# A convolution and a mixture of experts in one kernel, with the written-out order of all its steps made anew

## The chip, the cores and the metric

One core of one Trainium2 chip runs the whole program. The metric is device time in microseconds, the median of three runs: 1271.48 us for the kernel before (1271.06 to 1281.67).

## What is computed

The reference chains two parts, for 8 sequences of 3584 tokens with 192 channels, all in float32.

```
w = softmax(weight_gen, over 7 taps)                       # per token and head, 8 heads of 24 channels
out[b, s] = sum_k w[b, s, k] * x_pad[b, s + k]             # a causal convolution whose taps depend on the token
logits = out @ w_gate + modality_bias[modality_id]         # 8 experts
e = argmax(logits);  gate = softmax(logits)[e]
y = gate * (relu(out @ w1[e]) @ w2[e])                     # 192 -> 1024 -> 192, the chosen expert alone
```

The first three lines and the routing are called attention below, the last one pages.

## The kernel before

**Units and pages.** The 28672 tokens are worked on in 16 units of 1792 (128 partitions of 14 tokens), each unit in two halves of 7 tokens. A unit's rows, once convolved and routed, are scattered to the DRAM tensor `rows_scratch`, one region for each expert. As soon as enough units are in, full pages of 128 or 256 rows of one expert are loaded from there, go through the two layers, and each row is scattered to its place in the output. Of the pages' hidden layer, 225 groups of 1024 columns are worked on.

**Attention of a unit, by engine.**
- SP loads weights and tokens (`LU`, L369 to L382).
- VectorE and ScalarE make the softmax (`A`, `X`, `SM`, `SN`, `B`).
- VectorE multiplies tokens by tap weights, one large step of 128x1344 for each tap. In units 0 to 2 TensorE adds the products up (`M`, L584, then `S`, L596). From unit 3 on VectorE adds most of them itself: taps 0 and 3 start two sums, taps 4, 5 and 6 are made and added (`PQ`, L572, and `PA`, L617). Taps 1 and 2 are added to the first sum by DMAs that add as they write, issued by GpSimd (`DA`, L612). A last step merges the two sums (`PM`, L621). It must wait until the DMA of tap 2 has landed.
- ScalarE and VectorE split the result into two float16 parts (`H`, L627, and `L`, L635 and L636). TensorE turns the rows and multiplies by the gate (`T`, L645, and `G`, L669).
- VectorE chooses the expert in 7 short steps, `RA` (L677 to L695). TensorE counts ranks (`RR`, L706 and L708). VectorE makes each row's place in 6 more, `RB` (L715 to L729). GpSimd then scatters the unit in 14 indirect DMAs (`SC`, L741).
- VectorE makes the table that tells where the pages start, in 14 short steps on one partition (`TB`, L767 to L827). The letters RA, RB and TB with a unit's number name these short steps below.

**Weights.** At the start, the 8 experts' weights are loaded (`wld`, L863 to L865), squared and summed on ScalarE (`wsq`, L873), bounded on VectorE (`wmx`, L882), split in two float16 parts (`whi`, L921, and `wlo`, L925) and stored (`wst`, `wts`, L932 and L938).

**A page.** SP loads its rows turned (`PL`, L963) and its expert's weights (`PW`, L982). TensorE makes the hidden layer (`HM`, L1005), ScalarE and VectorE split it (`HA`, L1017, and `HL`, L1021), TensorE makes the output (`OM`, L1032 to L1034), ScalarE scales it (`OA`, L1039) and GpSimd scatters it (`OS`, L1044).

**The order.** No scheduler decides anything here: a string, `ORDER`, lists 3683 names such as `PQ.11.0.2` (tap 2 of the first half of unit 11), and a loop issues the steps in that order. Each engine gets its own steps in this order and works through them strictly one behind the other, waiting where a step's inputs are not there. So the string sets which work stands ahead of which on each engine. GpSimd has one queue for the scatters of rows (`SC`), the scatters of outputs (`OS`) and the adding DMAs (`DA`).

```
    for name in ORDER.split():
        name, _, after = name.partition("@")
        fn, *args = name.split(".")
```

Of the kernel before, what the change touches and what calls it, by code (L numbers as in the profile page):

```python
# [57 lines left out]
S.0.0.1 wsq.0.0 CA S.0.0.2 wsq.0.1 M.0.0.4 wld.1 CB XB.1 S.0.0.3 M.0.0.5 SI.0 wsq.1.0 A.1 S.0.0.4 wsq.1.1 M.0.0.6 X.1  # L58
wtr.1 M.0.1.0 S.0.0.5 SA.1.0 wld.2 wmx.1 BP.1 M.0.1.1 wsc.1 S.0.0.6 SA.1.1 wdg.1 SM.1 DA.0.1.1 M.0.1.2 SN.1 wbc.1
wsq.2.0 wld.3 B.1 S.0.1.2 wsf.1 H.0.0 M.0.1.3 wsq.2.1 L.0.0 S.0.1.3 whi.0.0 wsq.3.0 wlo.0.0 T.0.0 E.0.0 wsq.3.1 G.0.0  # L60
T.0.1 E.0.1 wpf.0 whi.0.1 wtr.3 M.0.1.4 G.0.1 whi.1.0 wmx.3 S.0.1.4 M.0.1.5 wsc.3 M.0.1.6 wpf.1 whi.1.1 wdg.3 wlo.0.1
LU.2 wbc.3 SB.1 S.0.1.5 wsf.3 SI.1 whi.2.0 M.1.0.0 wst.0 wld.4 T.0.2 S.0.1.6 M.1.0.1 E.0.2 wpf.2 whi.2.1 wlo.1.0 G.0.2
S.1.0.0 wsq.4.0 wts.0 M.1.0.2 XB.2 wsq.4.1 S.0.1.0 wlo.1.1 M.1.0.3 S.1.0.1 H.0.1 wlo.2.0 RI.0 wst.1 XM.2 S.1.0.2 BP.2
L.0.1 SA.2.0 wts.1 M.1.0.4 T.0.3 S.1.0.3 SA.2.1 M.1.0.5 E.0.3 wlo.2.1 S.1.0.4 SB.2 SI.2 wld.5 M.1.0.6 G.0.3 T.0.4
S.1.0.5 E.0.4 M.1.1.0 whi.3.0 wst.2 A.2 G.0.4 wsq.5.0 T.0.5 S.1.0.6 M.1.1.1 wts.2 E.0.5 wsq.5.1 wlo.3.0 G.0.5 T.0.6
S.1.1.0 E.0.6 M.1.1.2 wld.6 X.2 H.1.0 G.0.6 wtr.5 RA.0.0 S.1.1.1 wmx.5 RA.0.1 SM.2 wsc.5 wsq.6.0 RA.0.2 wdg.5 RA.0.3
L.1.0 wbc.5 S.1.1.2 RX.0 wsq.6.1 RA.0.4 M.1.1.3 SN.2 wsf.5 wpf.3 whi.3.1 RA.0.5 S.1.1.3 B.2 whi.4.0 RA.0.6 M.1.1.4 RR.0
wpf.4 whi.4.1 T.1.0 RB.0.0 S.1.1.4 wlo.3.1 SE.0 E.1.0 whi.5.0 RB.0.1 wst.3 M.1.1.5 T.1.1 wld.7 E.1.1 RB.0.2 S.1.1.5
wlo.4.0 wpf.5 whi.5.1 wts.3 wsq.7.0 RB.0.3 M.1.1.6 T.1.2 E.1.2 RB.0.4 S.1.1.6 wlo.4.1 wsq.7.1 RB.0.5 M.2.0.0 GW.0 wst.4
G.1.0 SC.0.0 wtr.7 H.1.1 wts.4 G.1.1 G.1.2 TB.0.0 wmx.7 S.2.0.0 TB.0.1 wlo.5.0 wsc.7 RI.1 SC.0.1 TB.0.2 wdg.7 TB.0.3  # L70
wbc.7 L.1.1 wsf.7 SC.0.2 TB.0.4 LU.3 wlo.5.1 T.1.3 E.1.3 SC.0.3 TB.0.5 M.2.0.1 G.1.3 T.1.4 wst.5 whi.6.0 SC.0.4 TB.0.6
M.2.0.2 S.2.0.1 E.1.4 wpf.6 whi.6.1 TB.0.7 SC.0.5 wts.5 wlo.6.0 G.1.4 T.1.5 S.2.0.2 TB.0.8 SC.0.6 E.1.5 wlo.6.1 whi.7.0
SC.0.7 TB.0.9 M.2.0.3 wst.6 G.1.5 TE.1 XB.3 T.1.6 wts.6 wpf.7 whi.7.1 TB.0.10 wlo.7.0 S.2.0.3 SC.0.8 E.1.6 TB.0.11
wlo.7.1 G.1.6 SC.0.9 RA.1.0 TB.0.12 RA.1.1 TB.0.13 RA.1.2 wst.7 M.2.0.4 SA.3.0 SC.0.10 RA.1.3 S.2.0.4 BP.3 RA.1.4 RX.1
M.2.0.5 SA.3.1 wts.7 SC.0.11 RA.1.5 M.2.0.6 S.2.0.5 SB.3 SC.0.12 RA.1.6 M.2.1.0 SI.3 RR.1 SC.0.13 RB.1.0 M.2.1.1 SE.1
S.2.0.6 RB.1.1 A.3 S.2.1.0 H.2.0 RB.1.2 M.2.1.2 X.3 S.2.1.1 RB.1.3 L.2.0 RB.1.4 SM.3 GW.1 S.2.1.2 SC.1.0 RB.1.5 M.2.1.3
SN.3 TB.1.0 B.3 T.2.0 SC.1.1 PW.0 S.2.1.3 E.2.0 PL.0 TB.1.1 M.2.1.4 SC.1.2 G.2.0 PW.1 T.2.1 PL.1 TB.1.2 E.2.1 M.2.1.5
S.2.1.4 SC.1.3 TB.1.3 M.2.1.6 PL.2 G.2.1 T.2.2 S.2.1.5 SC.1.4 E.2.2 TB.1.4 PQ.3.0.0 TB.1.5 PQ.3.0.1 SC.1.5 G.2.2 S.2.1.6
TB.1.6 PQ.3.0.3 PL.3 DA.3.0.1 TB.1.7 H.2.1 PQ.3.0.4 SC.1.6 RI.2 TB.1.8 L.2.1 SC.1.7 TB.1.9 PA.3.0.4 HM.0.0 TE.2 SC.1.8
TB.1.10 PQ.3.0.2 LU.4 TB.1.11 SC.1.9 PQ.3.0.5 T.2.3 HA.0.0 PL.4 HM.1.0 TB.1.12 PA.3.0.5 E.2.3 SC.1.10 GM.0 G.2.3 HL.0.0  # L80
T.2.4 HA.1.0 PL.5 E.2.4 TB.1.13 PQ.3.0.6 SC.1.11 OM.0.0 GM.1 HL.1.0 G.2.4 T.2.5 PW.2 PA.3.0.6 OA.0.0 DA.3.0.2 OM.1.0
E.2.5 XB.4 OS.0.0 PQ.3.1.0 G.2.5 T.2.6 PW.3 HM.2.0 OA.1.0 E.2.6 PQ.3.1.1 OS.1.0 PQ.3.1.3 G.2.6 HM.3.0 HA.2.0 DA.3.1.1
RA.2.0 GM.2 PQ.3.1.4 XM.4 PL.6 SC.1.12 HL.2.0 HA.3.0 GM.3 RA.2.1 SC.1.13 SA.4.0 OM.2.0 HL.3.0 RA.2.2 BP.4 RA.2.3
PA.3.1.4 RX.2 OM.3.0 SA.4.1 PW.4 RA.2.4 PM.3.0 HM.4.0 OA.2.0 PW.5 OA.3.0 OS.2.0 SB.4 RA.2.5 PQ.3.1.2 H.3.0 OS.3.0 HM.5.0
RA.2.6 PQ.3.1.5 HA.4.0 DA.3.1.2 SI.4 GM.4 HL.4.0 RR.2 HA.5.0 PL.7 RB.2.0 OM.4.0 L.3.0 GM.5 SE.2 PL.8 HL.5.0 T.3.0 E.3.0
RB.2.1 OM.5.0 A.4 PW.6 OA.4.0 PW.7 OS.4.0 PW.8 RB.2.2 T.3.1 X.4 PA.3.1.5 PL.9 HM.6.0 E.3.1 OA.5.0 RB.2.3 SM.4 PW.9
# [1058 lines left out]
```

## Time and profile before

| | |
|---|---|
| median of three runs | 1271.48 us |
| the profiled execution | 1273.82 us, of which 1272.1 us are the span of the trace |
| mean granted TensorE clock | 0.968 of full speed |
| TensorE (PE) busy | 1145.1 us, 90% of the span |
| VectorE (DVE) busy | 970.3 us, 76% |
| GpSimd (POOL) busy | 796.1 us, 63% |
| ScalarE (ACT) busy | 636.5 us, 50% |

The profile names engines PE, PEld (weight loads), DVE, ACT, POOL and SP. In the list of instructions in order of time a row gives start and duration in us, then engine, line, operation, what it writes and reads, and in brackets how long its engine stood idle before it and what ended that. The span of a POOL row for an indirect DMA is the time that GpSimd took to issue it, not the time of the transfer. A row of the table of stretches gives busy time in us and instructions (x) of each engine, then granted clock, share of the DMA engines and GB/s.

### The profile page before, as it was taken

To read this page: it belongs to the slowest core of one execution; us is meant where nothing else is said; L and a number is where in the kernel's file an instruction comes from. 1 tells how busy PE (TensorE), PEld (TensorE's weight loads), DVE (VectorE), ACT (ScalarE), POOL (GpSimd) and SP (SyncE) were. 2 spreads that over 40 slices of the span, in tenths; PEclk is the share of its full clock that TensorE was granted. 3 is DMA by queue.
4 is the path that set the end of the run, shared out by engine and by line. 5 is a ranking of instruction groups with operands and counts; after the bars stand their busy time and mean duration, and the time that the engine had idled before them with its cause. 6 is when DMAs were issued, how large, how long until landed. Compare 5 with 4: busy or idle time off the path is not lost.

```text
span 1272.1 us, 32564 instructions
## 1 busy us (share of the span) xinstructions
PE 1145.1 (90%) x13046; PEld 1031.2 (81%) x13046; DVE 970.3 (76%) x1187; ACT 636.5 (50%) x1109; POOL 796.1 (63%) x561
## 2 busy tenths in 40 slices
...
GB/s 307 199 293 297 257 178 231 250 178 244 152 101 165 131 219 194 179 109 190 117 229 159 168 121 176 111 170 164 162 107 120 98 89 105 103 43 49 49 137 110
DMA packets 177387, 205.49 MB, mean 162 GB/s; under 512 B 134864, under 2 KB 151500, under 8 KB 171857
## 3 DMA queue, kind: packets, MB, share of 16 engines
...
q8 instruction: 104, 1.70, 0.6%
...
## 4 chain that ended last, share of the span: by engine, by line
issue 27%; POOL 17%; DVE 9%; DMA 9%; PE 7%; ACT 1%; POOLq 1%; another core or an unknown queue 0%; SPq 0%; DVEq 0%; ACTq 0%
POOL out_dram L1044 9%; POOL rows_scratch L741 7%; DMA sum<-prod 5%; PE g L1005 3%; DVE lo L1021 2%; DMA rows_scratch<-rows,idx 2%; PE g L1034 1%; PE g L1032 1%; DVE tmp L572 1%; PE g L1033 1%; DMA out_dram<-ot,meta 1%; DVE sum L621 1%; DVE sum L617 1%; DMA xt<-in_x_dram 1%; POOL sum L612 1%
## 5 line engine op out<-in xcount | busy, mean ns | idle before, releaser
L1005 PE MATMUL g<-xT,w 128*128 128x256 f16 (+1 forms) x5800 | 539.8, 251 | 24.8 <-DVE lo L1021 8.3
L1044 POOL DMA_INDIRECT out_dram<-ot,meta x225 | 352.8, 1568 | 284.5 <-ACT ot L1039 233.2
L1005 PEld LDWEIGHTS <-w 128*128 128x128 f16 x5800 | 462.6, 99 | 63.2 <-issue 20.2
L741 POOL DMA_INDIRECT rows_scratch<-rows,idx x224 | 377.1, 1683 | 147.6 <-ACT rows L736 78.1
L1034 PE MATMUL g<-w,lo 128*128 128x192 f16 x1800 | 447.1, 248 | 12.2 <-DVE lo L1021 8.5
L1032 PE MATMUL g<-w,hi 128*128 128x192 f16 x1800 | 447.1, 248 | 9.0 <-ACT hi L1017 8.4
L1033 PE MATMUL g<-w,hi 128*128 128x192 f16 x1800 | 447.0, 248 | 0.8 <-issue 0.7
L1021 DVE SCALAR_TENSOR_TENSOR lo<-g,hi 128x1024 f16<-128x1024 f32 x225 | 273.4, 1216 | 199.3 <-ACT hi L1017 193.3
L1017 ACT ACTIVATE hi<-g 128x1024 f16<-128x1024 f32 x225 | 229.4, 1020 | 264.8 <-PE g L1005 229.6
L1034 PEld LDWEIGHTS <-lo 128*128 128x128 f16 x1800 | 177.9, 99 | 17.3 <-DVE lo L1021 12.0
L1032 PEld LDWEIGHTS <-hi 128*128 128x128 f16 x1800 | 177.8, 99 | 10.9 <-ACT hi L1017 8.8
L1033 PEld LDWEIGHTS <-hi 128*128 128x128 f16 x1800 | 178.0, 99 | 3.3 <-issue 1.8
L1039 ACT ACTIVATE ot<-g,gm 128x192 f32<-128x192 f32 x225 | 93.6, 416 | 145.2 <-PE g L1034 68.7
L596 PE MATMUL acc<-prod,ident 128*128 128x512 f32 (+1 forms) x240 | 107.6, 597 | 19.4 <-DVE prod L584 19.0
L617 DVE TENSOR_TENSOR sum<-sum,tmp 128x1344 f32<-128x1344 f32 x78 | 120.4, 1543 | 0.0
L572 DVE TENSOR_TENSOR tmp<-wt,xt 128x1344 f32<-128x1344 f32 x78 | 119.9, 1537 | 0.0
L649 ACT ACTIVATE xg<-gt 128x768 f16<-128x768 f16 x112 | 89.9, 803 | 44.5 <-PE gt L645 43.3
L596 PEld LDWEIGHTS acc<-prod,ident 128*128 128x128 f32 x240 | 47.7, 209 | 68.4 <-issue 57.8
L572 DVE TENSOR_TENSOR prod<-wt,xt 128x1344 f32<-128x1344 f32 x52 | 80.3, 1545 | 0.0
L572 DVE TENSOR_TENSOR sum<-wt,xt 128x1344 f32<-128x1344 f32 x52 | 80.2, 1543 | 0.0
L645 PE MATMUL gt<-ident,rows 128*128 128x128 f16 x672 | 60.3, 223 | 20.4 <-ACT rows L627 12.5
L621 DVE TENSOR_TENSOR sum<-sum,sum 128x1344 f32<-128x1344 f32 x26 | 40.2, 1548 | 49.8 <-DMA sum<-prod 49.8
...
## 6 DMA issues: line engine op xcount, KB each, us to landing
...
```

The costliest lines, as they stand in the source:

```text
L572: return nc.vector.tensor_tensor(to.rearrange("p t (h g) -> p t h g", h=H), win, xin, ALU.mult)
L596: nc.tensor.matmul(un[u]["psum", c][:, q], lhsT=ident32, rhs=un[u]["pr", c, k][:, q], start=(k == order[0]), stop=(k == order[-1]))
L617: return nc.vector.tensor_tensor(a, a, un[u]["tmp"], ALU.add)
L741: i = nc.gpsimd.indirect_dma_start(out=rows, out_offset=bass.IndirectOffsetOnAxis(ap=idx[:, j:j + 1], axis=0), in_=ri[:, j, 0:ROW // 2], i ...
L1005: nc.tensor.matmul(o, lhsT=wt[:, w0:w0 + P], rhs=xT[:, xi, :pt], start=(q * pt % 512 == 0 and j == 0), stop=(j == 4), skip_group_check=True)
L1017: return nc.scalar.activation(hi, pg["ps", grp], AF.Relu)
L1021: return nc.vector.scalar_tensor_tensor(lo, live[i]["ps", grp], 0.0, hi, op0=ALU.max, op1=ALU.subtract)
L1032: nc.tensor.matmul(ps, lhsT=hi, rhs=wt[:, w0:w0 + D], start=(f == 0), stop=False)
L1033: nc.tensor.matmul(ps, lhsT=hi, rhs=wt[:, w0 + D:w0 + 2 * D], start=False, stop=False)
L1034: nc.tensor.matmul(ps, lhsT=lo, rhs=wt[:, w0:w0 + D], start=False, stop=(f == NFT - 1))
L1039: nc.scalar.activation(ot, pg["out", t], AF.Copy, scale=pg["gm"][:, t:t + 1])
L1044: w = nc.gpsimd.indirect_dma_start(out=out, out_offset=bass.IndirectOffsetOnAxis(ap=pg["meta"][:, t, 1:2], axis=0), in_=pg["res", t], in_o ...
```

## The change

Only the string `ORDER` differs. The two strings hold the same 3683 names, so the same instructions run on the same data; the places of nearly all of them differ. Its first lines, cut:

```
@@ -55,240 +55,240 @@
 ORDER = """
 TE.0 A.0 X.0 SM.0 SN.0 B.0 SA.0.0 CL M.0.0.0 WP M.0.0.1 S.0.0.0 SA.0.1 CC LU.1 M.0.0.2 XB.0 SB.0 wld.0 BP.0 M.0.0.3
-S.0.0.1 wsq.0.0 CA S.0.0.2 wsq.0.1 M.0.0.4 wld.1 CB XB.1 S.0.0.3 M.0.0.5 SI.0 wsq.1.0 A.1 S.0.0.4 wsq.1.1 M.0.0.6 X.1
+S.0.0.1 CA S.0.0.2 M.0.0.4 wld.1 CB XB.1 S.0.0.3 M.0.0.5 SI.0 A.1 S.0.0.4 M.0.0.6 X.1 SA.1.0 M.0.1.0 S.0.0.5 wld.2 BP.1
...
```

On average, attention's names stand 15 or so places earlier and the pages' names 15 places later than before. When the merge of the first half of unit 14 comes, 140 groups of pages stand ahead of it in place of 142; from unit 6 on the number is one to three lower at each such merge.

**First place: VectorE around the merge of unit 11's first half.** `prod` is tap 2's product, which the adding DMA sends to the first sum; `tmp` and L617 are taps 5 and 6 and their adding; L1021 is a page's step; L677 to L692 are short rank steps of another unit; L621 is the merge. Before:

```order
L572 TENSOR_TENSOR prod<-wt,xt 128x1344
L572 TENSOR_TENSOR tmp<-wt,xt 128x1344
L572 TENSOR_TENSOR sum_10704<-wt,xt 128x1344
L1021 SCALAR_TENSOR_TENSOR lo<-g_10630,hi 128x1024
L617 TENSOR_TENSOR sum_10499<-sum_10499,tmp 128x1344
L677 SCALAR_TENSOR_TENSOR L<-lg,invg,bt 128x112
L572 TENSOR_TENSOR tmp<-wt,xt 128x1344
L1021 SCALAR_TENSOR_TENSOR lo<-g_10714,hi 128x1024
L679 SCALAR_TENSOR_TENSOR L<-lg,invg,L 128x112
L617 TENSOR_TENSOR sum_10499<-sum_10499,tmp 128x1344
L682 TENSOR_REDUCE gmx<-L 128x14
L621 TENSOR_TENSOR sum_10355<-sum_10355,sum_10499 128x1344
```

Now, with the short steps left out:

```order
L572 TENSOR_TENSOR prod<-wt,xt 128x1344
L572 TENSOR_TENSOR tmp<-wt,xt 128x1344
L1021 SCALAR_TENSOR_TENSOR lo<-g_10431,hi 128x1024
...
L617 TENSOR_TENSOR sum_10359<-sum_10359,tmp 128x1344
...
L572 TENSOR_TENSOR tmp<-wt,xt 128x1344
L1021 SCALAR_TENSOR_TENSOR lo<-g_10533,hi 128x1024
...
L617 TENSOR_TENSOR sum_10359<-sum_10359,tmp 128x1344
L1021 SCALAR_TENSOR_TENSOR lo<-g_10611,hi 128x1024
...
L572 TENSOR_TENSOR sum_10711<-wt,xt 128x1344
...
L572 TENSOR_TENSOR prod<-wt,xt 128x1344
L1021 SCALAR_TENSOR_TENSOR lo<-g_10682,hi 128x1024
...
L621 TENSOR_TENSOR sum_10237<-sum_10237,sum_10359 128x1344
```

Between tap 2's product and the merge stood five large steps and two of L1021, and now stand six and four. In GpSimd's queue, 232 scatters stood ahead of this merge's DMA, and now 230.

**Second place: VectorE while unit 0's table is made.** L767 to L797 are unit 0's table steps, L882 (`wmx`) and L894 belong to the last pair of experts, L925 and L584 are large steps, L677 is unit 1's first rank step. Unit 0's 14 scatters are GpSimd's work in these rows. Before:

```order
L767 SCALAR_TENSOR_TENSOR av<-nbase,off 1x8
L882 TENSOR_REDUCE wmx<-gt 4x1
L770 TENSOR_SCALAR fi<-av 1x8
L925 SCALAR_TENSOR_TENSOR hw<-wa,wsf,hw 128x3x512
...
L784 SCALAR_TENSOR_TENSOR rb<-cm,off 1x8
L584 TENSOR_TENSOR prod<-xt,wt 128x1344
L787 TENSOR_TENSOR rd<-rb 1x9
L584 TENSOR_TENSOR prod<-xt,wt 128x1344
L790 TENSOR_TENSOR spc_118<-g,rd 1x7x9
L925 SCALAR_TENSOR_TENSOR hw<-wa,wsf,hw 128x3x512
L793 TENSOR_REDUCE tb<-spc_118 1x7
```

Now:

```order
L781 TENSOR_TENSOR g<-slot_i,cm 1x63
L882 TENSOR_REDUCE wmx<-gt 4x1
L784 SCALAR_TENSOR_TENSOR rb<-cm,off 1x8
L584 TENSOR_TENSOR prod<-xt,wt 128x1344
L787 TENSOR_TENSOR rd<-rb 1x9
L894 TENSOR_TENSOR wdg<-ident_92,wsb 4x8
L790 TENSOR_TENSOR spc_118<-g,rd 1x7x9
...
L925 SCALAR_TENSOR_TENSOR hw<-wa,wsf,hw 128x3x512
L925 SCALAR_TENSOR_TENSOR hw<-wc,wsf,hw 128x8x192
L584 TENSOR_TENSOR prod<-xt,wt 128x1344 x3
L677 SCALAR_TENSOR_TENSOR L<-lg,invg,bt 128x112
```

Some of the table's steps now stand by threes, others still alone between two large steps. The step on `wmx` comes four table steps later. Behind the last table step five large steps follow one another, and unit 1's ranks come only behind these; all 14 scatters of unit 0 stand ahead of the first of the three L584 in the string.

**Third place: ScalarE where the weights of expert 4 arrive.** L873 squares these weights, L538 and L627 make the token biases and unit 0's second half. Before:

```order
L921 ACTIVATE hw<-wc,wsf 128x8x192
L873 ACTIVATE junk,wsum<-wa 128x1536
L538 ACTIVATE bt<-bias 128x112
L873 ACTIVATE junk,wsum<-wc 128x1536
L627 ACTIVATE rows_72<-acc,sf 128x7x192
L630 ACTIVATE rows_72<-ids 128x14
```

Now:

```order
L538 ACTIVATE bt<-bias 128x112
L921 ACTIVATE hw<-wa,wsf 128x3x512
L627 ACTIVATE rows_72<-acc,sf 128x7x192
...
L921 ACTIVATE hw<-wc,wsf 128x8x192
L649 ACTIVATE xg<-gt 128x768
L873 ACTIVATE junk,wsum<-wa 128x1536
L505 ACTIVATE junk,asum<-xt 128x1920
```

The biases and the unit's second half stood behind the wait for these weights, and now stand ahead of it.

More of the change, by code (lines that the diff above doesn't have):

```diff
@@ L57 @@
 TE.0 A.0 X.0 SM.0 SN.0 B.0 SA.0.0 CL M.0.0.0 WP M.0.0.1 S.0.0.0 SA.0.1 CC LU.1 M.0.0.2 XB.0 SB.0 wld.0 BP.0 M.0.0.3
[L58 to L86, printed above, removed]
@@ new lines @@
+M.0.1.1 wsq.0.0 S.0.0.6 SM.1 DA.0.1.1 SA.1.1 M.0.1.2 wld.3 M.0.1.3 SN.1 S.0.1.2 H.0.0 B.1 wsq.0.1 S.0.1.3 SB.1 L.0.0
+wsq.1.0 SI.1 wsq.1.1 T.0.0 E.0.0 wsq.2.0 wtr.1 G.0.0 wmx.1 wsc.1 M.0.1.4 wsq.2.1 wdg.1 M.0.1.5 S.0.1.4 M.0.1.6 wsq.3.0
+LU.2 wbc.1 M.1.0.0 S.0.1.5 wsf.1 whi.0.0 T.0.1 wsq.3.1 M.1.0.1 S.0.1.6 E.0.1 wlo.0.0 wpf.0 whi.0.1 G.0.1 T.0.2 S.0.1.0
+M.1.0.2 E.0.2 XB.2 whi.1.0 wlo.0.1 G.0.2 wtr.3 S.1.0.0 H.0.1 wmx.3 wst.0 wlo.1.0 wld.4 wsc.3 RI.0 wpf.1 S.1.0.1 whi.1.1
+wdg.3 L.0.1 wts.0 XM.2 BP.2 M.1.0.3 wbc.3 S.1.0.2 wsf.3 SA.2.0 M.1.0.4 whi.2.0 T.0.3 wlo.1.1 S.1.0.3 E.0.3 M.1.0.5 wpf.2
@@ new lines @@
+wst.1 whi.2.1 wts.1 G.0.3 T.0.4 S.1.0.4 M.1.0.6 E.0.4 wsq.4.0 wlo.2.0 G.0.4 T.0.5 SA.2.1 S.1.0.5 wld.5 M.1.1.0 E.0.5
+wlo.2.1 S.1.1.0 wsq.4.1 M.1.1.1 wst.2 whi.3.0 G.0.5 T.0.6 S.1.0.6 wts.2 A.2 E.0.6 wpf.3 whi.3.1 wlo.3.0 G.0.6 S.1.1.1
+X.2 wld.6 H.1.0 RA.0.0 SM.2 wsq.5.0 RA.0.1 L.1.0 SN.2 SB.2 RA.0.2 B.2 wsq.5.1 T.1.0 RA.0.3 M.1.1.2 RX.0 E.1.0 SI.2 wtr.5
+RA.0.4 M.1.1.3 S.1.1.2 RA.0.5 wmx.5 RA.0.6 wsc.5 M.1.1.4 RB.0.0 RR.0 wsq.6.0 wdg.5 wlo.3.1 wbc.5 S.1.1.3 SE.0 wsf.5
+whi.4.0 RB.0.1 wst.3 M.1.1.5 wld.7 T.1.1 wsq.6.1 S.1.1.4 RB.0.2 wlo.4.0 E.1.1 wts.3 wpf.4 RB.0.3 whi.4.1 M.1.1.6 T.1.2
@@ new lines @@
+S.1.1.5 E.1.2 RB.0.4 wlo.4.1 GW.0 whi.5.0 SC.0.0 S.1.1.6 RB.0.5 M.2.0.0 wst.4 wpf.5 whi.5.1 wts.4 SC.0.1 TB.0.0 wlo.5.0
+G.1.0 S.2.0.0 H.1.1 SC.0.2 TB.0.1 wlo.5.1 wsq.7.0 G.1.1 SC.0.3 G.1.2 RI.1 TB.0.2 L.1.1 wst.5 wts.5 wsq.7.1 SC.0.4 TB.0.3
+M.2.0.1 wtr.7 SC.0.5 TB.0.4 wmx.7 S.2.0.1 TB.0.5 M.2.0.2 wsc.7 SC.0.6 TB.0.6 wdg.7 TB.0.7 M.2.0.3 LU.3 wbc.7 SC.0.7
+S.2.0.2 wsf.7 TB.0.8 M.2.0.4 whi.6.0 SC.0.8 TB.0.9 wpf.6 TB.0.10 wlo.6.0 TE.1 whi.6.1 T.1.3 S.2.0.3 SC.0.9 E.1.3 TB.0.11
+wlo.6.1 whi.7.0 G.1.3 T.1.4 SC.0.10 S.2.0.4 TB.0.12 M.2.0.5 wst.6 E.1.4 wts.6 wpf.7 whi.7.1 SC.0.11 TB.0.13 wlo.7.0
@@ new lines @@
+PQ.4.0.1 SC.2.6 TB.2.7 PQ.4.0.3 DA.4.0.1 T.3.3 TB.2.8 PQ.4.0.4 HA.7.0 PL.10 SC.2.7 E.3.3 HM.8.0 HL.7.0 GM.7 PL.11 XB.5
+TB.2.9 PA.4.0.4 SC.2.8 TE.3 G.3.3 T.3.4 HA.8.0 OM.7.0 TB.2.10 PQ.4.0.2 E.3.4 GM.8 SC.2.9 HL.8.0 G.3.4 T.3.5 HM.9.0
+OA.7.0 E.3.5 TB.2.11 PQ.4.0.5 OS.7.0 PW.11 SA.5.0 TB.2.12 BP.5 G.3.5 TB.2.13 PL.12 PA.4.0.5 T.3.6 OM.8.0 SC.2.10
+PQ.4.1.0 HA.9.0 E.3.6 PW.12 SC.2.11 HL.9.0 OA.8.0 GM.9 SA.5.1 G.3.6 RA.3.0 DA.4.0.2 OM.9.0 PQ.4.0.6 PL.13 OS.8.0 SB.5
+RA.3.1 PA.4.0.6 HM.10.0 OA.9.0 PW.13 SI.5 SC.2.12 RA.3.2 PQ.4.1.1 HA.10.0 OS.9.0 RA.3.3 PQ.4.1.3 RX.3 GM.10 DA.4.1.1
```

419 lines of the change are left out of this document (214 added, 205 removed).

## The prediction

> **What bounds the kernel now.** I read the busy times first, in four stretches: until the first page, while weights and the first pages mix, the long middle in which attention and pages run side by side, and the pages that are left.
>
> ```profile
> 0.00:166.00 166.00, 121.05 (x496) 61.34 (x496) 135.34 (x156) 100.56 (x161) 62.68 (x78) 0.93 0.80 269
> 166.00:352.00 186.00, 161.70 (x2423) 156.58 (x2424) 170.13 (x211) 100.44 (x184) 140.63 (x86) 0.95 0.80 203
> 352.00:960.00 608.00, 562.70 (x6347) 525.62 (x6345) 552.87 (x680) 317.90 (x559) 484.61 (x296) 0.97 0.66 156
> 960.00:1272.10 312.10, 299.62 (x3787) 287.64 (x3784) 111.98 (x143) 117.58 (x207) 108.19 (x104) 1.00 0.34 90
> ```
>
> The first column of busy times is PE's. It idles 45.0, 24.3, 45.3 and 12.5 us in the four, 127 in all. Its work is the same in both kernels, so the end can move only by as much as this idle time does. In the last stretch PE is nearly full and VectorE (third column) is not: whatever attention leaves over is paid there at PE's pace, one group of a page for each L1021:
>
> ```profile
> 1063.73 1.23 DVE L1021 SCALAR_TENSOR_TENSOR lo<-g,hi 128x1024 f16<-128x1024 f32 x1 [2.94 <-ACT hi L1017]
> 1067.90 1.22 DVE L1021 SCALAR_TENSOR_TENSOR lo<-g,hi 128x1024 f16<-128x1024 f32 x1 [2.94 <-ACT hi L1017]
> ```
>
> That is 4.17 us a group. Second, the waits: what stops VectorE in the middle is one thing, the merge of the two sums that waits for the adding DMA.
>
> ```profile
> DVE sum L621 <- DMA sum<-prod: 49.8, 9, 11.0
> ```
>
> Third, I followed the longest of these nine waits, in unit 11, on VectorE:
>
> ```profile
> 670.44 1.54 DVE L572 TENSOR_TENSOR prod<-wt,xt 128x1344 f32<-128x1344 f32 x1
> 671.91 1.54 DVE L572 TENSOR_TENSOR tmp<-wt,xt 128x1344 f32<-128x1344 f32 x1
> 673.38 1.54 DVE L572 TENSOR_TENSOR sum<-wt,xt 128x1344 f32<-128x1344 f32 x1
> 674.85 1.20 DVE L1021 SCALAR_TENSOR_TENSOR lo<-g,hi 128x1024 f16<-128x1024 f32 x1
> 675.98 1.53 DVE L617 TENSOR_TENSOR sum<-sum,tmp 128x1344 f32<-128x1344 f32 x1
> ...
> 693.65 1.56 DVE L621 TENSOR_TENSOR sum<-sum,sum 128x1344 f32<-128x1344 f32 x1 [11.04 <-DMA sum<-prod]
> ```
>
> and in the same time on GpSimd:
>
> ```profile
> 671.20 4.62 POOL L1044 DMA_INDIRECT out_dram<-ot,meta  x1 [0.30 <-ACT ot L1039]
> 676.12 2.25 POOL L1044 DMA_INDIRECT out_dram<-ot,meta  x1 [0.30 <-ACT gm L990]
> 678.68 1.76 POOL L1044 DMA_INDIRECT out_dram<-ot,meta  x1 [0.30 <-ACT hi L1017]
> ...
> 683.28 0.99 POOL L612 DMA_DIRECT2D sum<-prod  x1
> ```
>
> The product is done at 671.98, but five scatters stand ahead of its DMA and GpSimd gets to it at 683.28. How long scatters take (shortest, median, longest in ns), and what stands on VectorE beside the longest of them:
>
> ```profile
> L741 POOL DMA_INDIRECT rows_scratch<-rows,idx x224: 967/1260/14300, 113.4 to 1046.8; - x112
> 118.06 14.30 POOL L741 DMA_INDIRECT rows_scratch<-rows,idx  x1 [0.30 <-issue]
> ```
>
> ```profile
> 119.43 0.15 DVE L784 SCALAR_TENSOR_TENSOR rb<-cm,off 1x8 f32<-1x8 f32 x1
> ...
> 122.66 1.80 DVE L925 SCALAR_TENSOR_TENSOR hw<-wa,wsf,hw 128x1536 f16<-128x1536 f32 x1
> 124.39 0.21 DVE L793 TENSOR_REDUCE tb<-spc 1x7 int32<-1x70 f32 x1
> ...
> 131.44 0.32 DVE L677 SCALAR_TENSOR_TENSOR L<-lg,invg,bt 128x112 f32<-128x112 f32 x1
> ```
>
> From 119.43 to 131.44 large steps and single table steps alternate, seven of each, and the scatter gets in only with the first rank step: it ends at 132.36, 0.97 us (the shortest time) after 131.39. In unit 11 the scatter at 671.20 likewise ends 0.97 us after 674.85, when three large steps in a row have given way to L1021. So large steps shut scatters out, a lone table step hardly opens, GpSimd falls behind, the DMA goes late, the merge waits. PE then starves:
>
> ```profile
> 696.40 1.01 PE L1005 MATMUL g<-xT,w 128*128 128x256 f16 x4 [8.32 <-DVE lo L1021]
> 893.73 0.29 PE L645 MATMUL gt<-ident,rows 128*128 128x128 f16 x1 [5.81 <-ACT rows L627]
> ```
>
> The second row follows unit 14's merge, the last of the long ones. So the sum runs up to that merge, and PE's remaining work follows it.
>
> **The change part by part.** No instruction is added or removed.
>
> *Pages moved back.* At unit 14's merge two groups fewer are done: 2 x 4.17 = 8.3 us more of PE's work behind it. VectorE has two L1021 (674.85 to 675.98, 1.13 us each) less and 1.9 us of attention more ahead of it, net -0.4. Together **+8.0**. Nothing hides it, since PE is full behind that merge.
>
> *Merge waits.* From tap 2's product to the merge I count VectorE's steps in both orders, from start to next start: 1.47 us for a large step, 1.13 for L1021, some 0.2 for a short one. Unit 11 had 5 x 1.47 + 2 x 1.13 + short ones = 10.2, and now has 6 x 1.47 + 4 x 1.13 + short ones = 14.5. For the first halves of units 3 to 15, before and now: 19.1/18.6, 19.3/20.0, 14.3/14.5, 10.2/14.6, 11.1/11.6, 11.7/11.5, 14.1/11.6, 14.4/11.6, 10.2/14.5, 12.6/14.3, 11.7/11.9, 11.3/15.8, 9.7/11.9. (The second halves have more and never waited.) The other waits are in units 3, 6, 8, 9, 12, 13, 14 and 15:
>
> ```profile
> 195.38 1.56 DVE L621 TENSOR_TENSOR sum<-sum,sum 128x1344 f32<-128x1344 f32 x1 [6.78 <-DMA sum<-prod]
> 374.16 1.56 DVE L621 TENSOR_TENSOR sum<-sum,sum 128x1344 f32<-128x1344 f32 x1 [7.81 <-DMA sum<-prod]
> 500.82 1.58 DVE L621 TENSOR_TENSOR sum<-sum,sum 128x1344 f32<-128x1344 f32 x1 [2.47 <-DMA sum<-prod]
> 564.07 1.56 DVE L621 TENSOR_TENSOR sum<-sum,sum 128x1344 f32<-128x1344 f32 x1 [1.81 <-DMA sum<-prod]
> 757.69 1.56 DVE L621 TENSOR_TENSOR sum<-sum,sum 128x1344 f32<-128x1344 f32 x1 [3.89 <-DMA sum<-prod]
> 822.45 1.56 DVE L621 TENSOR_TENSOR sum<-sum,sum 128x1344 f32<-128x1344 f32 x1 [5.75 <-DMA sum<-prod]
> 890.66 1.56 DVE L621 TENSOR_TENSOR sum<-sum,sum 128x1344 f32<-128x1344 f32 x1 [7.83 <-DMA sum<-prod]
> 951.60 1.56 DVE L621 TENSOR_TENSOR sum<-sum,sum 128x1344 f32<-128x1344 f32 x1 [2.44 <-DMA sum<-prod]
> ```
>
> If the DMA lands as long after its product as before, each wait changes by the change of its distance: units 3, 6, 8, 9 come to 7.3, 3.4, 2.7, 4.3; unit 10 to an estimated 1 (it lost 2.8 of a slack that no row gives); units 11 to 14 to 6.7, 2.2, 5.5, 3.3. To unit 14 that is 36.4 in place of 47.4: **-11.0**. Bounds: 0, if GpSimd falls back as much as the merge does, and -47.4, if every DMA lands in time. GpSimd's queue speaks for a gain: ahead of the tap-2 DMAs of units 7 to 14 stand two or three scatters fewer than before. But in units 11 to 15, where four of the five gain distance, one or two scatters more stand between product and DMA. So I keep the count by distance.
>
> *The start.* Four VectorE waits lie in the weights' preparation:
>
> ```profile
> 49.57 0.28 DVE L882 TENSOR_REDUCE wmx<-gt 4x1 f32<-4x128 f32 x1 [1.47 <-PE gt L878]
> ...
> 69.84 0.29 DVE L549 COPY_PREDICATED bt<-mt,bias 128x112 f32<-128x112 int32 x1 [4.19 <-ACT bt L538]
> 73.15 0.69 DVE L635 SCALAR_TENSOR_TENSOR rows<-acc,sf,rows 128x448 f16<-128x448 f32 x1 [3.02 <-ACT rows L627]
> ...
> 113.52 0.28 DVE L882 TENSOR_REDUCE wmx<-gt 4x1 f32<-4x128 f32 x1 [3.88 <-PE gt L878]
> ```
>
> The middle two stood behind ScalarE's wait for expert 4's weights (third place); now they stand ahead of it, and what stands behind it, a copy for the gate, is wanted only by rank steps 10 us of VectorE work later. That is 7.2. The last goes as `wmx` comes 6.9 us of VectorE work later: 3.9. Of 11.1 I take **-8**: the first `wmx`, 8.9 us of work later, still waits for squares that ScalarE now does behind unit 1's sums. Bounds: -3 and -11.
>
> Against the profiled execution: 1273.8 + 8.0 - 11.0 - 8 = 1262.8. It stands 2.3 above the median, so I forecast **1260.5 us**, 0.9% faster.
>
> **A rule weighed.** The scatter at 118.06 lasted far longer than any one VectorE step (1.80 us is the longest shown). The Trainium skill, "SBUF — State Buffer", section "SBUF: two separate sides", says that the pair of ports which both engines share is locked for one whole instruction, and that a blocked transfer goes "blocked until DVE-end + ~115 ns". By that rule a scatter would slip in behind any large step; this trace does not agree, with its 14.30 us across seven of them.
>
> **Rivals.**
> - *No change, by let-in at each step's end* (the rule above). A scatter then takes at most 1.80 + 0.97, some 2.8 us, whatever stands beside it, the late DMAs come from something else, a busy queue or the landing, and distances measured against large steps decide nothing. What is left is +8.0 and -8: 1271.5. For it: half of L741's scatters take 1.26 or less. Against: the 14.30, and 4.62 in unit 11.
> - *All merges in time.* If two or three scatters fewer are worth their full time at every merge, the waits go. PE gives back its gaps behind them, which are smaller than VectorE's waits (8.32 for 11.04, 5.81 for 7.83, so some three quarters of 47.4, 36): 1273.8 + 8 - 36 - 8 - 2.3 = 1236, in part up to 1252. Against: the distances of units 8, 9, 10 and 13 did not grow.
> - *Slower: unit 0 is shut out for longer.* First page's load and first matmul:
>
> ```profile
> 152.10 1.30 SPq L963 DMA_TRANSPOSE xT<-rows_scratch  x1
> 166.32 3.66 PE L1005 MATMUL g<-xT,w 128*128 128x128 f16 x40 [3.78 <-DMA wt<-in_weight_gen_dram]
> ```
>
> The load waits for unit 0's last scatter. The change does not bunch all of unit 0's steps: several table steps (second place) still stand alone, and behind the last one come five large steps, two of L925 (1.73 from 122.66 to 124.39) and three of 1.47, 7.9 us in all. If a second shut-out of 14.3 falls there, the first page comes 14.3 later and the start's gain is gone: 1273.8 + 8 + 14.3 - 11 - 2.3 = 1283, and 1294 with the merges as late as before. It decides from the point where unit 0's last scatter ends after some 150 us.
>
> **How the numbers follow.** Forecast 0.50 (its own range 1253 to 1268), all in time 0.18, no change 0.16, slower 0.16. A measurement of this kernel tells about 1% (12.7 us) from no change. Below 1258.8 lie the second case and 0.20 of the first: faster 0.38. Above 1284.2 lies most of the last: slower 0.12. Within 1%: 0.50. The range, 1243 to 1279, leaves out half of the second case and most of the last.
>
> **What would show it.** The total of L621's waits for the DMA should fall from 49.8 to 35 to 40, with units 6, 11 and 14 lowest against before; VectorE's waits at L549 and L635 near 70 us should be gone; the first matmul of L1005 should start before 166; the last stretch, after attention, should hold two groups more. I am wrong if L621's total stays near 50 or falls below 20, or if the first page starts later than 170.

## The result, and the profile after

The changed kernel took 1269.72 us in the median of 12 runs (1251.39 to 1283.95), the kernel before 1277.75 us in 12 runs on the same chip (1271.06 to 1284.19). The ratio is 0.9893, with a 95% interval of 0.9852 to 0.9933. In a second comparison (`after_again` below) it is 0.9871 (0.9821 to 0.9921): 1250.69 us against 1267.91. So the change is about 1.1 to 1.3% faster, as forecast in size. The sum behind the forecast does not hold up so well, as the rows show.

The ratio of 0.9893 leaves out six of the changed kernel's 12 runs as disturbed, those over 1.5% above its fastest; with all of them in, the medians lie 0.6% apart. The profile taken with this comparison is of one of the six, so the one read here is the changed kernel's second, `after_again` below (1248.73 us). Its string is broken into more lines, so every line number stands 4 higher: the merge L621 is L625, the scatter L741 is L745, a page's L1005 is L1009.

First the same stretches as before, with the same columns.

```profile
0.00:166.00 166.00, 131.95 (x651) 74.10 (x652) 151.09 (x176) 111.42 (x182) 65.55 (x88) 0.91 0.92 295
166.00:352.00 186.00, 159.78 (x2404) 156.30 (x2403) 170.68 (x214) 97.68 (x183) 152.65 (x86) 0.94 0.77 192
352.00:960.00 608.00, 573.45 (x6464) 538.39 (x6462) 559.54 (x690) 322.34 (x561) 501.42 (x301) 0.97 0.66 158
```

The great difference is in the first row: VectorE (third busy time) does 151.09 us of work in the first 166 us, where it did 135.34, so 15.8 more, and PE 10.9 more. What VectorE waited for in the first 166 us (total, times, longest), before and then after:

```profile
DVE wmx L882 <- PE gt L878: 10.6, 3, 5.3
DVE prod L584 <- PE acc L596: 5.8, 5, 1.9
DVE bt L549 <- ACT bt L538: 4.2, 1, 4.2
...
DVE rows L635 <- ACT rows L627: 3.0, 1, 3.0
```

```profile
DVE prod L588 <- PE acc L600: 5.9, 4, 1.9
DVE mx L533 <- DMA wt<-in_weight_gen_dram: 4.3, 1, 4.3
DVE wmx L886 <- PE gt L882: 2.5, 1, 2.5
```

The two waits of 4.2 and 3.0 us are gone, and of 10.6 us at `wmx` 2.5 are left: 15.3 us in these three groups. Behind `wmx` stand ScalarE's squares. Before, ScalarE asked for them ahead of the weights' arrival, and stood still for that. Its largest wait in the first 115 us before was this; no such row is left after.

```profile
ACT junk L873 <- DMA wa<-in_moe_w_dram: 22.3, 3, 9.1
```

The first page's matmul, at 166.32 before:

```profile
146.27 4.02 PE L1009 MATMUL g<-xT,w 128*128 128x128 f16 x40 [3.46 <-DVE cm L781]
```

Then the merges. The total of their waits for the adding DMA (49.8 before), and its rows:

```profile
DVE sum L625 <- DMA sum<-prod: 43.7, 9, 9.0
```

```profile
236.44 1.56 DVE L625 TENSOR_TENSOR sum<-sum,sum 128x1344 f32<-128x1344 f32 x1 [9.03 <-DMA sum<-prod]
...
666.33 1.56 DVE L625 TENSOR_TENSOR sum<-sum,sum 128x1344 f32<-128x1344 f32 x1 [7.47 <-DMA sum<-prod]
...
789.40 1.56 DVE L625 TENSOR_TENSOR sum<-sum,sum 128x1344 f32<-128x1344 f32 x1 [7.99 <-DMA sum<-prod]
860.50 1.56 DVE L625 TENSOR_TENSOR sum<-sum,sum 128x1344 f32<-128x1344 f32 x1 [7.91 <-DMA sum<-prod]
```

These are units 4, 11, 13 and 14. Unit 14 waits as long as before (7.83), unit 13 longer (5.75), and unit 4, which did not wait at all, now waits 9.03. In the first profile of the change the total is 59.9 us.

### The profile page after: what moved, and what is told of

Read it like the earlier page. It is cut to its first block, busy times and chain, and to the rows that moved or that the text cites. A ratio compares the mean times of both kernels' runs of the same rounds, so it can differ in the third digit from the quotient of the medians.

```text
span 1282.2 us, 32581 instructions
## 1 busy us (share of the span) xinstructions
PE 1149.8 (90%) x13046; PEld 1038.7 (81%) x13046; DVE 970.4 (76%) x1187; ACT 637.1 (50%) x1109; POOL 800.9 (62%) x561
## 5 line engine op out<-in xcount | busy, mean ns | idle before, releaser
L1005 PE MATMUL g<-xT,w 128*128 128x256 f16 (+1 forms) x5800 | 547.3, 253 | 17.1 <-DMA w<-weights_scratch 8.2
L1044 POOL DMA_INDIRECT out_dram<-ot,meta x225 | 346.0, 1538 | 299.1 <-ACT ot L1039 246.7
L1005 PEld LDWEIGHTS <-w 128*128 128x128 f16 x5800 | 468.2, 100 | 56.3 <-issue 10.6
L741 POOL DMA_INDIRECT rows_scratch<-rows,idx x224 | 388.2, 1733 | 141.8 <-ACT rows L736 73.5
L1021 DVE SCALAR_TENSOR_TENSOR lo<-g,hi 128x1024 f16<-128x1024 f32 x225 | 273.5, 1216 | 216.1 <-ACT hi L1017 212.0
L596 PE MATMUL acc<-prod,ident 128*128 128x512 f32 (+1 forms) x240 | 104.3, 582 | 18.1 <-DVE prod L584 18.1
L617 DVE TENSOR_TENSOR sum<-sum,tmp 128x1344 f32<-128x1344 f32 x78 | 120.4, 1543 | 0.0
L621 DVE TENSOR_TENSOR sum<-sum,sum 128x1344 f32<-128x1344 f32 x26 | 40.3, 1550 | 59.9 <-DMA sum<-prod 59.9
L627 ACT ACTIVATE rows<-sum,sf 128x1344 f16<-128x1344 f32 x26 | 36.7, 1413 | 73.3 <-DVE sum L621 57.0
```

Of the source, the lines that this page charges most:

```text
L596: nc.tensor.matmul(un[u]["psum", c][:, q], lhsT=ident32, rhs=un[u]["pr", c, k][:, q], start=(k == order[0]), stop=(k == order[-1]))
L617: return nc.vector.tensor_tensor(a, a, un[u]["tmp"], ALU.add)
L741: i = nc.gpsimd.indirect_dma_start(out=rows, out_offset=bass.IndirectOffsetOnAxis(ap=idx[:, j:j + 1], axis=0), in_=ri[:, j, 0:ROW // 2], i ...
L1005: nc.tensor.matmul(o, lhsT=wt[:, w0:w0 + P], rhs=xT[:, xi, :pt], start=(q * pt % 512 == 0 and j == 0), stop=(j == 4), skip_group_check=True)
L1021: return nc.vector.scalar_tensor_tensor(lo, live[i]["ps", grp], 0.0, hi, op0=ALU.max, op1=ALU.subtract)
L1044: w = nc.gpsimd.indirect_dma_start(out=out, out_offset=bass.IndirectOffsetOnAxis(ap=pg["meta"][:, t, 1:2], axis=0), in_=pg["res", t], in_o ...
```

## The experiments

Twelve kernels ran, in four groups, each beside the kernel before on one chip. Times compare only within a group, as ratios: the kernel before alone has medians from 1264 to 1278 us on these chips, and single profiles of its one order lie 14 us apart (below). "B" is the order of before, "A" that of the change; `HM.0.0` is the first page's first matmul, `SC.0.0` unit 0's first scatter. The first four ran together.

### The change again, and its two halves

```diff
 after_again:  A
 start_new:    A up to HM.0.0, the rest as in B
 start_old:    B up to HM.0.0, the rest as in A
```

> The changed kernel once more, with nothing edited, beside the kernels below and profiled in a run that is not disturbed. Reading of the first profile of the change: its first page's matmul starts at 145.9 us, 20.4 earlier than the 166.32 of before, but the waits of L621 for the DMA of tap 2 add up to 59.9 us (49.8 before), so nearly all that the end gained comes from the start. Theory (start): this profile repeats it, with the first L1005 at 144 to 148, L621's waits at 45 to 65 us, and a time 0.985 to 0.993 of before. Rival (merges, as the prediction had it): the 59.9 belong to that one execution, and here L621's waits come to 35 to 40 us.

> The change's order up to the first page's first matmul (HM.0.0), and behind it the order of before. Theory (start): the start gains some 20 us and all of it reaches the end, less what the order behind, made for a later start, does not take up: 0.984 to 0.990 of before (-13 to -20 us), at least as fast as the whole change. Rival (the prediction's sum): the start is worth 8 us, 0.994 of before, and the merges the other 11.

> The order of before up to the first page's first matmul, and behind it the change's. Theory (start): without the new start only the pages that stand later and the merges are left, +8 us and 0 to -5, so 1.000 to 1.008 of before, and the first L1005 at some 166. Rival (the prediction's sum): +8.0 - 11.0 = -3 us, 0.998, with L621's waits at 35 to 40 us; if all merges were in time, 0.98.

Measured: `after_again` 0.9871 (0.9821 to 0.9921), `start_new` 0.988 (0.983 to 0.993), `start_old` 1.0035 (1.0003 to 1.0067). The start carries all of it, as the first theory has it, and what the later order does comes to nothing or a little loss. The 43.7 us of `after_again` lie between the marks of the theory (45 to 65) and the rival (35 to 40). Milestones of the profiled executions, in us:

| | first page's matmul | merge of unit 3 | of unit 6 | of unit 14 | end of span |
|---|---|---|---|---|---|
| before | 166.3 | 195.4 | 374.2 | 890.7 | 1272.1 |
| before, second profile | 166.2 | 192.7 | 374.3 | 881.4 | 1258.0 |
| change (`after_again`) | 146.3 | 171.4 | 350.1 | 860.5 | 1247.0 |
| `start_new` | 145.4 | 181.1 | 358.6 | 872.1 | 1249.8 |
| `start_old` | 165.7 | 189.2 | 368.3 | 875.1 | 1260.5 |
| `weights_new` (below) | 155.3 | 181.8 | 370.2 | 877.5 | 1257.5 |
| `weights_old` (below) | 158.5 | 184.5 | 362.7 | 892.0 | 1283.2 |
| `first_squares` (below) | 160.2 | 186.7 | 382.3 | 892.2 | 1268.8 |

In the stretch behind unit 14's merge the two later orders differ as forecast. The change first, then `start_new`, whose later order is that of before:

```profile
860.50:1247.00 386.50, 370.74 (x4581) 356.37 (x4580) 178.18 (x224) 153.09 (x264) 161.20 (x140) 0.98 0.38 98
```

```profile
872.10:1249.80 377.70, 361.52 (x4493) 346.52 (x4493) 177.03 (x225) 151.22 (x261) 163.74 (x138) 0.99 0.41 99
```

88 matmuls and 9.2 us of PE's work more are left behind that merge: the two groups (VectorE has 86 of a page's L1021 there in place of 84). The stretch is 8.8 us longer.

`start_new` loses elsewhere what it does not lose here: its pages stand early, as in B, and VectorE stands before the first of them. Its line numbers are 5 higher; this is L1021:

```profile
167.35 1.23 DVE L1026 SCALAR_TENSOR_TENSOR lo<-g,hi 128x1024 f16<-128x1024 f32 x1 [9.01 <-ACT hi L1022]
```

That is most of the 9.7 us by which its unit 3 is later than the change's (181.1 and 171.4). So in these two profiles, with the early start, attention ahead of pages is worth about what the two pages cost at the end.

### What a merge wait is worth

```diff
 def add_far(u, c, k):
+    if (c, k) == (0, 2) and u > 2:
+        return
```

> The changed kernel without the 13 adding DMAs of tap 2 in the first halves of units 3 to 15: the product is still made, but is left out of the sum, and the merge has only the earlier DMA of tap 1 to wait for. This prices the merge waits at the end of the program. Theory: VectorE's waits at L621 fall from some 50 to 60 us to under 10, and TensorE gives back three quarters of those up to unit 14's merge, some 30 to 40 us: 0.955 to 0.967 of before. Rival: TensorE has enough pages at hand to bridge most of these waits, its idle time behind them has other causes, and the time falls by under 12 us (0.980 or more of before).

Measured 1.005 (1.0008 to 1.0092), which is no price: with a tap missing other experts are chosen, the pages came to 231 groups in place of 225, and the last six stand behind all others. So I compare the 225th group's L1021 with that of the same order, and the waits up to unit 14's merge. Without the DMAs (numbers 2 higher), then with them (4 higher):

```profile
1216.82 1.23 DVE L1023 SCALAR_TENSOR_TENSOR lo<-g,hi 128x1024 f16<-128x1024 f32 x1 [2.99 <-ACT hi L1019]
```

```profile
DVE sum L623 <- DMA sum<-prod: 16.6, 5, 6.8
```

```profile
1236.11 1.23 DVE L1025 SCALAR_TENSOR_TENSOR lo<-g,hi 128x1024 f16<-128x1024 f32 x1 [2.99 <-ACT hi L1021]
```

```profile
DVE sum L625 <- DMA sum<-prod: 41.2, 8, 9.0
```

The waits fell by 24.6 us and the group came 19.3 earlier, 0.78 us for each microsecond of waiting. The waits are real costs, then, but the price is rough: it comes from one pair of profiles, the rows on the pages are not the same ones, and GpSimd has 13 DMAs fewer to issue besides. I had expected the waits under 10 us. Of the 16.6 left, 6.8 are in unit 13's first half, at tap 1's DMA, and nearly all others in second halves, which hardly waited before and now come sooner. The gain of 19.3 us lies between what the two expectations named, under 12 us and 30 to 40.

### Three tries to bring the DMA forward

All three start from A. The first two ran in one group with `weights_new` and `weights_old` of the next section, the third with `squares_late`.

```diff
 tap2_early:  -  PQ.u.0.4 PA.u.0.4 ... PQ.u.0.2 ... DA.u.0.2      (u = 3 to 15)
              +  PQ.u.0.2 PQ.u.0.4 DA.u.0.2 PA.u.0.4 ...
 da2_next:    -  PQ.u.0.2 ... SC ... OS ... DA.u.0.2
              +  PQ.u.0.2 DA.u.0.2 ... SC ... OS ...
 scat_back:   -  DA.u.0.1 ... SC ... SC ... DA.u.0.2
              +  DA.u.0.1 ... DA.u.0.2 SC SC
```

> The changed kernel with tap 2's product ahead of tap 4's in the first halves of units 3 to 15, and its DMA right behind tap 4's product: one or two large steps (1.5 to 2.9 us) more between product and merge, and the DMA one to three scatters earlier in GpSimd's queue. Theory (distance, the prediction's count): each of the waits goes by 1.5 to 2.9 us or more, L621 in all from 43.7 to 18 to 28 us, 0.970 to 0.980 of before. Rival (GpSimd is behind by more than that, and the DMA goes out no earlier against the merge): 35 to 45 us stay, 0.985 to 0.990.

> The changed kernel with the DMA of tap 2 directly behind its product in the order, in the first halves of units 3 to 15: the same distance on VectorE, but none of the scatters that stood between product and DMA in GpSimd's queue. Theory (scatters in between make the DMA late): these one to four scatters at 1.3 to 4 us each are gone from the DMA's way, L621's waits fall from 43.7 to 10 to 22 us, 0.970 to 0.978 of before. Rival (the DMA's landing, or a backlog from earlier scatters, decides): waits of 33 us or more, 0.985 to 0.990. A second rival: GpSimd now waits for the product with scatters queued behind it, these come later, and the gain at L621 is given back elsewhere, 0.983 or more with waits under 25 us.

> The changed kernel with the scatters of rows that stand between the DMAs of taps 1 and 2 (one to seven, mostly two or three, in the first halves of units 3 to 15) put directly behind the DMA of tap 2. VectorE's order is the same, and so are the places of the two DMAs. In the profiles so far the merge starts some 4.5 to 5 us after the DMA's issue ends, and the issue starts 2 to 23 us after its product. Theory (scatters in the way make the DMA late): L621's waits fall from 43.7 to 8 to 22 us, the issue comes on average 4 us closer to its product, 0.972 to 0.980 of before. Rival (the scatters' lateness goes elsewhere): the waits fall as much, but rows and pages come later and TensorE idles for these instead, 0.985 or more. Second rival (an older backlog): waits of 30 us or more, 0.985 to 0.990.

Measured: `tap2_early` 1.007 (1.0031 to 1.0108) with 35.6 us of L621's waits in all (30.0 for the DMA, and one of 5.6 for which the profile names nothing), `da2_next` 0.9894 (0.9856 to 0.9932) with 37.3, `scat_back` 0.9988 (0.995 to 1.0026) with 33.0. The waits are those of the rivals (an older backlog), the time of `scat_back` that of its first rival. None beats the change: `da2_next` is as fast, and `tap2_early` loses the whole gain and more, which I expected of neither theory. `scat_back` ran on a chip on which the change did not. GpSimd's rows show what came in place of the merge waits. In unit 4 of `tap2_early`:

```profile
214.60 0.97 POOL L612 DMA_DIRECT2D sum<-prod  x1
231.56 0.88 POOL L612 DMA_DIRECT2D sum<-prod  x1 [15.98 <-DMA sum<-prod]
```

Both DMAs add to the same sum, so tap 2's waits until tap 1's has landed; here GpSimd stood still for that for 15.98 us, with all scatters queued behind. Over the program it stands idle 82.5 us ahead of its adding DMAs in this kernel, 41.1 in `da2_next`, 43.5 in `scat_back` and 8.2 in the change's second profile (22.1 in its first; the idle time of all rows of L612 added up). So the merge waits that went came back as idle GpSimd. That this idle time is what `tap2_early` lost is likely but not shown: `da2_next` and `scat_back` have as much of it as each other, and one is as fast as the change and the other as slow as before. None of the three places for the DMA was better than that of the change. The runs also show that scatters between product and DMA are not the whole of the lateness: with none of them left there in the order, the DMA of `da2_next` went out 6.9 us after its product in unit 11 (15.4 in the change), but still 16.5 after it in unit 14 (18.0) and 19.0 in unit 13 (13.9), behind scatters and tap 1's DMA, which stood ahead of it.

### The start, taken apart

```diff
 weights_new:    A up to SC.0.0, the rest as in B
 weights_old:    B up to SC.0.0, the rest as in A
 squares_late:   B, with one edit:
-  wsq.4.0 ... XB.2 wsq.4.1 ... H.0.1 ... RI.0 ... E.0.3 ... E.0.4
+  XB.2 ... H.0.1 ... RI.0 ... E.0.3 wsq.4.0 ... E.0.4 wsq.4.1
 first_squares:  A up to the squares of expert 3's weights, the rest as in B
```

> The change's order up to unit 0's first scatter, the order of before from there on, so the weights and unit 0's ranks as changed, and the bunch of unit 0's table steps not. In the change's start, unit 0's last rank step comes 11.5 us earlier (86.2 for 97.7), its first scatter another 5.5 and its last another 5.4 earlier. Theory (ranks first): this kernel has the 11.5, first L1005 at 153 to 157 and 0.990 to 0.994 of before, with one long shut-out among unit 0's scatters as before. Rival (the bunch of table steps does it): first L1005 at 160 or later and 0.995 or more.

> The order of before up to unit 0's first scatter, the change's from there on: the bunch of table steps without the earlier ranks. Theory (ranks first, then the bunch): unit 0's 14 scatters take 5 to 6 us less than the 33.1 of before, first L1005 at 156 to 162, and with what the later order takes (+0.35 % in the kernel with the old start) 0.996 to 1.000 of before. Rival (the bunch does it): first L1005 at 150 or earlier, 0.990.

> The order of before, with only the two squares of expert 4's weights on ScalarE moved behind unit 0's second half, so that the token biases and this half no longer stand behind the wait for these weights: one of the change's moves by itself. Theory (what stands behind that wait costs its full length): VectorE's waits of 4.2 and 3.0 us near 70 us go, unit 0's last rank step comes 7 us earlier (90 to 92 for 97.7), the first L1005 at 157 to 160, and 0.993 to 0.996 of before. Rival (the squares make something else late, as the bounds of the next experts' weights): the last rank step at 95 or later, 0.998 or more.

> The change's order until the squares of expert 3's weights and unit 1's second product, the order of before from there on: only the first wave of squares (experts 0 to 3) later, not the move of expert 4's. ScalarE waits 9.1 us at 24.3 for the first weights before, and VectorE 5.3 at 33.2 for their maximum; with the change's start these are 0 and 2.5. Theory (every square that was asked for too early cost ScalarE, so the first wave counts as well as expert 4's): unit 0's last rank step at 91 to 95 for 97.7, 0.994 to 0.998 of before. Rival (the 11.5 us come from the move of expert 4's squares together with what stands behind them): the last rank step at 96.5 or later, 0.998 or more. A second one (the first wave is most of it): 90 or earlier, 0.993 or less.

Measured: `weights_new` 0.9884 (0.9841 to 0.9926), with unit 0's last rank step at 85.9 and the first page at 155.3. That is the first theory and a little better: the weights' part alone, without the bunch of table steps, is as good as the whole start. `weights_old` 1.0076 (1.004 to 1.0112), first page at 158.5: the bunch does bring the page nearly 8 us forward as expected, but the end does not follow, and both theories miss.

`squares_late` 1.0011 (0.9973 to 1.0049): the rival. The waits of 4.2 and 3.0 us at L549 and L635 went, and others took their place, behind the copies for the gate and the softmax of unit 2, which now stood behind the squares on ScalarE:

```profile
87.37 0.33 DVE L677 SCALAR_TENSOR_TENSOR L<-lg,invg,bt 128x112 f32<-128x112 f32 x1 [3.71 <-PE lg L669]
...
95.25 0.85 DVE L554 RECIPROCAL sm<-sm 128x112 f32<-128x112 f32 x1 [2.20 <-ACT sm L545]
```

The last rank step ends at 97.3 against 97.7. `first_squares` 1.0001 (0.996 to 1.0042): the last rank step ends 4.9 us earlier, at 92.8, as expected, and the first page comes 6 us earlier, but nothing of it is left at the end, which is the time of the rival. In its profile it is lost between the merges of units 3 and 6 (195.6 us, before 178.8), where PE waits for page weights. PE's rows for that stretch, before and then `first_squares`:

```profile
PE g L1005 <- DMA w<-weights_scratch: 5.3, 3, 2.0
```

```profile
PE g L1005 <- DMA w<-weights_scratch: 15.0, 4, 5.4
...
PE g L1005 <- DMA xT<-rows_scratch: 3.9, 2, 3.0
```

### Before, once more

```diff
 before_again: B
```

> The kernel before with nothing edited, for a second profile: how much the waits of L621 differ between executions of one order. The two profiles of the change have 59.9 and 43.7 us. Theory (each wait depends on how the scatters of that execution fall): L621's waits come out between 40 and 60 us with other units among the nine, the first page's matmul at 165 to 167 as before. Rival (the waits are fixed by the order): the nine units of before again, each within 1 us.

Measured 1.0009 (0.9966 to 1.0053) against its own copy, as it must be. The profiled execution took 1259.77 us, 14.05 less than the first one (1273.82); whether both ran on the same chip is not known. L621's waits:

```profile
DVE sum L621 <- DMA sum<-prod: 42.3, 9, 9.3
```

The same nine units wait, so the rival is right on that; but unit 13 has 0.64 us in place of 5.75 and unit 3 has 4.21 in place of 6.78. Here the order fixes which units wait, and chance moves single ones by up to 5 us. The change's two profiles agree less: unit 8 waits 7.64 us in the first and not at all in `after_again`. A total of 49.8 therefore can't be told from 42.3, nor from the change's 43.7.

## Why the prediction was right in its sum and wrong in two of its terms

**Pages moved back, +8.0: right.** The measured stretch is 8.8 us longer, PE's work in it 9.2.

**The start, -8: the mechanism right, the size not.** The waits at L549 and L635 went as forecast, 7.2 us. At `wmx` I had only the waits of 1.47 and 3.88 us in hand, and took the first as kept. The largest of the three I had passed over:

```profile
33.22 0.28 DVE L882 TENSOR_REDUCE wmx<-gt 4x1 f32<-4x128 f32 x1 [5.25 <-PE gt L878]
```

In all 15.3 us of these waits went and VectorE did 15.8 us more by 166 us. Unit 0's last rank step moved by 11.5 us (97.7 to 86.2). At the end the start is worth 1 - 0.988 = 1.2% of 1267.91, some 15 us (9 to 22), where I had 8. The third place of the change, on which I put 7.2 us of it, gives nothing by itself (`squares_late`): that "a copy for the gate, is wanted only by rank steps 10 us of VectorE work later" was wrong for an order in which that copy stands behind squares that still wait. It holds in the change, where all squares come later and no wait of ScalarE for weights is left.

**Merge waits, -11.0: wrong.** The failed step is "If the DMA lands as long after its product as before". The distances came out as counted: 14.5 us in unit 11, 15.8 in unit 14, and in all 13 units within 0.9 us of the forecast. The DMA did not keep its delay. For units 11 and 14 of `after_again`, tap 2's product on VectorE:

```profile
642.78 1.54 DVE L576 TENSOR_TENSOR prod<-wt,xt 128x1344 f32<-128x1344 f32 x1
```

```profile
835.23 1.54 DVE L576 TENSOR_TENSOR prod<-wt,xt 128x1344 f32<-128x1344 f32 x1
```

and its DMA on GpSimd, with what stood ahead of it in unit 11:

```profile
642.13 4.58 POOL L745 DMA_INDIRECT rows_scratch<-rows,idx  x1 [0.30 <-issue]
...
654.27 4.13 POOL L745 DMA_INDIRECT rows_scratch<-rows,idx  x1 [0.30 <-issue]
658.71 0.97 POOL L1048 DMA_INDIRECT out_dram<-ot,meta  x1 [0.31 <-issue]
659.68 0.99 POOL L616 DMA_DIRECT2D sum<-prod  x1
```

```profile
854.73 0.99 POOL L616 DMA_DIRECT2D sum<-prod  x1
```

Before, the rows of unit 11 stand in the prediction. Those of unit 14 were:

```profile
869.90 1.54 DVE L572 TENSOR_TENSOR prod<-wt,xt 128x1344 f32<-128x1344 f32 x1
```

```profile
884.93 0.99 POOL L612 DMA_DIRECT2D sum<-prod  x1
```

From the product's end to the DMA's start are 15.4 us in unit 11 (644.32 to 659.68; before 11.3) and 18.0 us in unit 14 (836.77 to 854.73; before 13.5). In unit 14, where the merge comes 4.4 us later after the product, GpSimd fell back by 4.5, and the wait stayed at 7.9 us. That is the bound that the prediction named for zero, "if GpSimd falls back as much as the merge does". The line on the one or two scatters more between product and DMA in units 11 to 15 spoke for it, and I did not follow it.

Unit 11 is another case. There GpSimd fell back by 4.1 and the merge by 3.9, and yet the wait fell from 11.04 to 7.47, close to the 6.7 that I had forecast. What changed is the last part of the wait, from the end of the DMA's issue to the merge: 9.4 us before, 5.7 now, and 7.6 in the second profile of before. So the prediction put the longest wait down to scatters alone where a slow landing had a share in it, and that wait came out near its forecast because two changes cancelled. What makes this part long in unit 11 is open.

Over the 13 units, the time from product to DMA changed by anything from -11.0 us (unit 3) to +13.7 (unit 4, from 9.6 to 23.3, which made a new wait of 9.03). Much of this comes with the order: `start_old`, which has the change's later order behind the old start, repeats the change's times within 0.1 us in 12 of the 13 units and within 1.1 in unit 4. `weights_old`, which has it too, does so in units 6, 7, 10 and 14, and is up to 5.6 us off elsewhere.

Up to unit 14's merge the waits come to 41.2 us where the prediction had 36.4, against 47.4 in the one profile of before and 39.9 in the other (42.3 less unit 15's 2.4). So a gain can't be told from zero within what these show. The total of 43.7 falls between the prediction's two marks (35 to 40, and "if L621's total stays near 50"), the first profile's 59.9 lies above both, and unit 14, named as one of the lowest against before, did not fall.

**The sum.** With measured sizes, from `start_new` to the whole change: +9.2 for the pages, -9.0 for the wait at the first page, which `start_new` has and the change has not, -2.0 for the merges (43.2 to 41.2), together -1.8; the medians differ by 1.4 us, which by itself could not be told from nothing. With the start's 15 that makes 16 to 17 us, 1.3%. So the 0.9% forecast came from a merge term 9 us too good, a start term 7 us too small, and a gain of 9 us at the first page that I had not seen, since I costed the exchange of attention and pages only at unit 14. That the total still came within 6 us is luck in part: the merge term erred to the fast side and the other two to the slow side.

**The rivals.** The slower one named its place rightly: behind unit 0's last table step one scatter was shut out across two steps of L925 and three of L584 (here 4 higher), 7.9 us by the count.

```profile
117.08 1.80 DVE L929 SCALAR_TENSOR_TENSOR hw<-wa,wsf,hw 128x1536 f16<-128x1536 f32 x1
118.81 1.80 DVE L929 SCALAR_TENSOR_TENSOR hw<-wc,wsf,hw 128x1536 f16<-128x1536 f32 x1
120.54 4.47 DVE L588 TENSOR_TENSOR prod<-xt,wt 128x1344 f32<-128x1344 f32 x3
124.95 0.32 DVE L681 SCALAR_TENSOR_TENSOR L<-lg,invg,bt 128x112 f32<-128x112 f32 x1
```

```profile
118.23 7.64 POOL L745 DMA_INDIRECT rows_scratch<-rows,idx  x1 [0.30 <-issue]
126.17 1.83 POOL L745 DMA_INDIRECT rows_scratch<-rows,idx  x1 [0.31 <-issue]
```

It ends at 125.87, 0.92 us after the first rank step starts. But unit 0's last scatter ends at 128.0, far from the 150 from which it would have decided, because the scatters start at 96.4 in place of 113.4. The let-in at each step's end, as the prediction took it from the rule of the Trainium skill, "SBUF — State Buffer", section "SBUF: two separate sides", fails on this row too: by it the scatter would have ended within some 2.8 us. The forecast of no change that went with it missed as well. "All merges in time" did not happen, but its price for a wait, some three quarters, agrees with the rough 0.78 above.

**What stays open.** Starts that are 6 to 8 us earlier at the first page (`first_squares`, `weights_old`) brought nothing at the end, one with 11 us (`weights_new`) as much as one with 21 (`start_new`). For `first_squares` the profile names page weights that come late; this is read from one execution and was not tried. That the later order costs 0.35% with the old start in one group and 0.76% with the bunch in another was not settled either: in the profile of `weights_old` L621 waits 56.2 us with the same later order that has 43.0 in `start_old`, on another chip.
